# Moving the closing conditional between the last experts, gate tiles to VectorE, and weight splits to two engines

## The chip, the core and the metric

One core of one Trainium2 chip runs the whole kernel. The metric is the device time of one execution in microseconds; less is better. Three timed runs of the kernel before gave 894.11, 895.85 and 896.01 us, median 895.85. The profile is of one further execution.

## What is computed

Three layers in a row, all in float32: attention with 4 sink positions and a window of 128 keys; a dense mixture, in which every token passes all four experts; and a routed mixture, in which each token passes one of eight.

```python
x = attention(q, k, v)                      # 1536 tokens x 512
out = 0
for e in range(4):                          # dense layer, F = 1024
    h = maximum(x @ w1[e], 0)
    out += p[:, e:e+1] * (h @ w2[e])
x = out
idx = argmax(cos(x, expert_emb) / tau)      # routed layer
gate = softmax(...)[idx]
for e in range(8):
    m = idx == e
    out[m] = gate[m] * (maximum(x[m] @ w1[e], 0) @ w2[e])
```

## The kernel before

Every float32 operand of a matmul is split in two float32r halves: the high half is a cast, the low half the difference from the original. Three matmuls (high x high, high x low, low x high: SPLIT3) then give the product. Weights are loaded as raw chunks of 512 KB by SP; each chunk is split in two pieces, and each piece costs one cast (line 676 on ScalarE, 678 on another engine) and one subtraction (line 682).

**Attention and the first dense products.** The attention has a narrow path, always emitted, and a general path in a conditional at line 1464, taken only for other sinks and windows and never here. Around that conditional lie the first products of expert 0 of the dense layer, on the first 512 tokens: Moe1.first makes products 0 to 3 with their activation (ScalarE relu at line 1003, VectorE difference at 1004), then products 4 and 5 without, which stay in the two PSUM buffers of the pool psa. Moe1.again, in the conditional, makes them anew if the general path has rewritten x. Moe1.rest activates 4 and 5 and makes 6 and 7. Moe1.splits issues the weight pieces that belong to a product, on ScalarE and VectorE, and the loads that follow from freed buffers.

**Routing.** While the dense layer's last expert runs, class Route ranks tokens by expert. For each group of token tiles, gate_a to gate_e work out the gate: gate_a an inverse root on GpSimd and VectorE, gate_b and gate_c the softmax, gate_d two 128 x 96 tiles a token tile (line 933, on GpSimd), gate_e one matmul a token tile into gtab (line 940). Two groups of four come early; the last four token tiles are a joined group (a = 8, n = 4) whose gates are done late, inside the routed layer's first two slots, as the list gates_late returns.

**Routed layer.** Tokens of one expert are worked on in slots of 128. Moe2.slot is one slot: 24 matmuls of the first layer in two halves (hooks a0 to a3, b0 to b3), relu on ScalarE (1204), transposes of each half (1210, hooks t0, t1) with a copy on ScalarE (1212) and the low half on VectorE (1213), then eight products of three matmuls (1219, hooks c0 to c7). At a hook other work is emitted, so the hooks set the order on each engine's queue. An object Fill hands out the pieces of the next expert's weights one by one: the cast of a piece at one call, its subtraction and the load that its buffer allows at the next. The function busy (line 1340) chooses the engines of piece i out of 16: cast on VectorE for i = 2, 6, 11 and on ScalarE otherwise, subtraction on GpSimd for i = 0, 3, 6, 9, 12 and on VectorE otherwise.

Tokens come by an indirect DMA issued by GpSimd (gather, line 1103) into xg, are transposed by TensorE (1117) and split by ScalarE (1121) and VectorE (1122). A slot's result is scaled on ScalarE (1163) and scattered by GpSimd (1164) in flush, called at hook a3 of the next slot; gate and row numbers of a finished slot are copied by current (1173, 1174) before that.

Moe2.begin is slot 0 of expert 0, Moe2.second its slot 1, and paced every other. An expert's further slots lie in conditionals (more_slots, line 1346) that are taken by token count; in this data experts 2, 3 and 5 need one slot, 0, 1 and 7 two, 4 and 6 three. Expert e computes from one of two weight stores while the other is filled for expert e + 1. After the last slot comes flush, and after that a conditional at line 1390 whose body, overflow, would work off experts with more than three slots; it is not taken here. Where a conditional is not taken, each engine's sequencer branches over its body, waits for the engine's own outstanding work and raises its semaphores by what the body would have added. The branch hint for line 1390 is announced in announce_rest, early in the routed layer.

In the profile PE is TensorE, PEld its weight loads, DVE VectorE, ACT ScalarE, POOL GpSimd, SP the DMA queue's engine; a q behind a name is that engine's sequencer.

Of the kernel before, what the change touches and what calls it, by code (L numbers as in the profile page):

```python
# [14 lines left out]
ALU = mybir.AluOpType  # L15
# [10 lines left out]
NT = N // P  # L26
# [695 lines left out]
class Route:  # L722
# [204 lines left out]
    def gate_d(s, g):  # L927
        C, M = s.C, E2 * NT
        g["gc"] = []
        for j in range(g["n"]):  # L930
            b = s.rl.tile([P, 2, M], F32R, tag="s3", name="s3", bufs=4)
            for i, v in enumerate((g["gh"].bitcast(F32), g["gl"])):
                s.nc.gpsimd.tensor_scalar(b[:, i], C.col, g["col"][:, j : j + 1], v[:, j : j + 1], ALU.is_equal, ALU.mult)
            g["gc"].append(b)

    def gate_e(s, g):
# [46 lines left out]
class Moe1:  # L983
# [37 lines left out]

    def first(s):

        s.hs, s.ph = [], []
        for f in range(s.HELD):
            s.splits(f, False)
            s.hs.append(s.tile(f))
            s.hidden(0, f, s.hs[f])
            s.splits(f, True)
        for f in (s.HELD, s.HELD + 1):  # L1030
            s.splits(f, False)
            s.ph.append(s.product(0, f, s.psa))

    HELD = 4

    def again(s, ps):
        for f, t in enumerate(s.hs):
            s.activate(s.product(0, f, ps), t)
        for i, ph in enumerate(s.ph):
            s.again_product(0, s.HELD + i, ph)  # L1040

    def rest(s):
        for f in range(s.HELD, 8):
            s.hs.append(s.tile(f))
            i = f - s.HELD
            if i < 2:
                s.activate(s.ph[i], s.hs[f])
            else:
                s.splits(f, False)
                s.hidden(0, f, s.hs[f])  # L1050
            s.splits(f, True)


def moe1(m, nc, wts, w1, w2, wA, acc, C, pos, route, then, early):
# [94 lines left out]
class Moe2:  # L1149
# [113 lines left out]
    def second(s, w, x, fl, more):  # L1263

        hooks = {
            "start": [lambda: fl(1)],
            "a0": [lambda: fl(1)],
            "a2": [lambda: fl(1)],
            "a3": [s.flush, lambda: fl(1)],
            "t0": [lambda: fl(2)],  # L1270
            "b1": [lambda: fl(1)],
            "b2": [lambda: fl(1)],
            "t1": [lambda: fl(1)],
            "c2": [lambda: fl(2)],
            "c3": [lambda: fl(2)],
            "c5": [fl.rest, lambda: s.current(0, 1)],
        }
        for n, f in more.items():
            hooks[n] = hooks.get(n, []) + f
        s.slot(x, w, hooks)  # L1280
# [36 lines left out]
    def run(s, psT, sp, wts, hx, wAB):  # L1317
        nc, tc, R = s.nc, s.tc, s.R
        V, A, G = nc.vector, nc.scalar, nc.gpsimd
        s.psT = psT  # L1320
        x0, x1 = [sp.tile([P, 2, 4, P], F32R, name=f"xt{i}") for i in range(2)]
        xg = [sp.tile([P, D], F32, name=f"xg{i}") for i in range(2)]
        for t in xg:
            G.memset(t, 0.0)
        for c in s.stream[5:7]:
            c.buf = hx.tile([P, 1024], F32, tag="h", name="raw")
            wts.bufs.append(c.buf)
            c.load()
        nb = len(wts.bufs)
        for i, c in enumerate(s.stream[nb:]):  # L1330
            c.buf = wts.bufs[i % nb]

        def items_for(e):
            r = []
            for i in range(8 * (e - 1), 8 * e):
                a, b = s.stream[i].parts()
                r += [a + (None,), b + (s.stream[i + nb].load if i + nb < len(s.stream) else None,)]
            return r

        def busy(i):  # L1340
            return V if i in (2, 6, 11) else A, V if i % 3 or i == 15 else G


        def more_slots(e, w, ks, c):

            with ExitStack() as nest:  # L1346
                for k in ks:
                    nest.enter_context(tc.If(c > 0, label=f"more{e}_{k}", preferred_fallthrough_block=True))
                    n, more = [], {}
                    if k < ks[-1]:  # L1350
                        more["a2"] = [lambda: n.append(R.has(e, k + 1))]
                        s.gather(xg[1], e, k + 1)
                        more["c2"] = [s.split_tokens(xg[1], x1)]
                    s.paced(e, k, x1, w, Fill([], busy), more)
                    c = n[0] if n else None

        for e in range(E2):
            w = wAB[e % 2]
            nxt = e + 1 < E2
            its = items_for(e + 1) if nxt else []  # L1360
            if e == 0:
                s.gather(xg[0], 1, 0)
                s.gather(xg[1], 0, 2)
                g = s.late
                n = []
                s.second(
                    w,
                    s.x1,
                    Fill(its, busy),
                    {  # L1370
                        "start": g[1:2],
                        "a1": g[2:3],
                        "a3": g[3:4],
                        "a0": [s.announce_rest],
                        "b1": [lambda: n.append(R.has(0, 2))],
                        "c2": [s.split_tokens(xg[0], x0)],
                        "c3": g[4:5],
                        "c4": g[5:] + [s.split_tokens(xg[1], x1)],
                    },
                )  # L1380
                more_slots(0, w, range(2, CAP), n[0])
            else:
                n = []
                s.gather(xg[1], e, 1)
                if nxt:
                    s.gather(xg[0], e + 1, 0)
                s.paced(e, 0, x0, w, Fill(its, busy), {"a2": [lambda: n.append(R.has(e, 1))], "c2": [s.split_tokens(xg[1], x1)], "c4": [s.split_tokens(xg[0], x0)] if nxt else []})
                more_slots(e, w, range(1, CAP), n[0])
        s.flush()
        with tc.If(s.rest > 0, label="rest", preferred_fallthrough_block=True):  # L1390
            s.overflow(wts, wAB[0], xg[0], x0)

    def announce_rest(s):

# [3 lines left out]
    def overflow(s, wts, w, t, x):  # L1398

        nc, R = s.nc, s.R  # L1400
        for e in range(E2):
            with ExitStack() as nest:
                for k in range(CAP, NT):
                    nest.enter_context(s.tc.If(R.has(e, k) > 0))
                    if k == CAP:
                        for i, ch in enumerate(wts.chunks(*s.wb[e], w)):
                            ch.buf = wts.bufs[i % len(wts.bufs)]
                            ch.load()
                            for hi, lo in ch.parts():
                                hi(nc.scalar)  # L1410
                                lo(nc.vector)
                    s.gather(t, e, k)
                    s.split_tokens(t, x)()
                    s.slot(x, w, {})
                    s.scatter(s.po[0], s.at(R.gates, e, k), s.at(R.idx, e, k))

    def split_tokens(s, t, o):
        def f():
# [125 lines left out]
```

## Time and profile before

| | us |
|---|---|
| median of three runs | 895.85 (894.11 to 896.01) |
| the profiled execution's own time | 898.2 |
| its span in the profile | 896.4 |
| VectorE busy | 417.4 (47%) |
| ScalarE busy | 302.1 (34%) |
| GpSimd busy | 193.1 (22%) |
| mean granted TensorE clock | 0.987 of full |

Times in the profile count from the span's start. The dense products begin at 124 us, the routed layer's first slot near 678 us, and the last matmul ends near 887 us. A row of the timeline is a run of like instructions on one engine; the brackets at its end say how long the engine was idle before it and what ended that. An idle engine costs time only if TensorE, or the end of the kernel, waits for it.

### The profile page before, as it was taken

How to read it: one execution, taken by the hardware profiler on the slowest of the kernel's cores; microseconds unless marked ns; L12 is line 12 of the kernel's file. 1: busy time of each engine (PE TensorE's matmuls, PEld its weight loads, DVE VectorE, ACT ScalarE, POOL GpSimd, SP SyncE). 2: the span in 40 equal slices, each digit the busy share in tenths (PEclk: the TensorE clock that was granted, in tenths of full speed). 3: DMA queues.
4: the chain of work that ended last, by engine and by line, in shares of the span. 5: the costliest groups of instructions: out<-in, count | busy, mean ns of one | idle time of the engine just before them, and what ended most of it. 6: DMA issues, size and time to landing. Idle time of an engine off the chain costs nothing. (4 is left out here: it accounts for less than half of the span.)

```text
span 896.4 us, 11797 instructions
## 1 busy us (share of the span) xinstructions
PE 869.3 (97%) x4266; PEld 681.0 (76%) x4266; DVE 417.4 (47%) x1003; ACT 302.1 (34%) x662; POOL 193.1 (22%) x291
## 2 busy tenths in 40 slices
PE   8999999999999999999999999999999799999995
PEld 6676777878888888888888888888887577777774
DVE  5787753121233121233121234858646768937510
ACT  5787852010302010302010303111233557636421
POOL 4576510000000000000000000030223846726310
PEclk8999999999999999999999999999999999999998
DMA  7567110030022000023000022101345577946200
GB/s 135 107 137 154 46 46 2 1 119 1 0 94 94 1 0 1 1 94 94 1 1 1 0 71 84 58 0 48 118 136 170 163 254 222 307 141 205 70 32 24
DMA packets 84400, 72.47 MB, mean 81 GB/s; under 512 B 43860, under 2 KB 68436, under 8 KB 84328
## 3 DMA queue, kind: packets, MB, share of 16 engines
q1 hardware_dynamic: 81448, 65.25, 25.0%
q0 software_dynamic: 2880, 6.30, 2.1%
q8 instruction: 40, 0.66, 0.3%
q14 instruction: 32, 0.26, 0.1%
HBM read 67.58 MB, written 7.09 MB: 83 GB/s over the span
## 5 line engine op out<-in xcount | busy, mean ns | idle before, releaser
L998 PE MATMUL ph<-x,wA 128*128 128x512 f32 x1152 | 273.0, 397 | 1.5 <-DVE h L1004 1.5
L1082 PE MATMUL po<-wA,h 128*128 128x512 f32 x1152 | 273.3, 396 | 0.0
L998 PEld LDWEIGHTS ph<-x,wA 128*128 128x128 f32 x1152 | 216.5, 188 | 54.2 <-DVE h L1004 1.9
L1082 PEld LDWEIGHTS po<-wA,h 128*128 128x128 f32 x1152 | 215.1, 188 | 51.7
L1003 ACT ACTIVATE h<-ph 128x512 fp32r<-128x512 f32 x96 | 57.4, 598 | 389.4 <-PE ph L998 384.1
L1004 DVE SCALAR_TENSOR_TENSOR h<-ph,h 128x512 fp32r<-128x512 f32 x96 | 66.4, 692 | 175.9 <-ACT h L1003 175.9
L60 POOL TENSOR_TENSOR gn<-gn,rss 128x4 f32<-128x4 f32 x9 | 1.8, 198 | 444.1 <-DVE gn L58 443.6
L682 DVE TENSOR_TENSOR wA<-raw,wA 128x512 fp32r<-128x512 f32 x107 | 77.3, 750 | 2.5 <-ACT wA L676 1.7
L1092 DVE SCALAR_TENSOR_TENSOR acc<-po,pr,acc 128x512 f32<-128x512 f32 x36 | 27.0, 750 | 109.9 <-PE po L1082 109.9
L676 ACT CAST wA<-raw 128x512 fp32r<-128x512 f32 x115 | 65.5, 618 | 4.0 <-DMA raw<-in_moe_w_dram 3.6
L408 POOL TENSOR_TENSOR P<-P,r 128x264 f32<-128x264 f32 (+1 forms) x87 | 54.2, 647 | 43.9 <-DVE r L403 24.5
L1219 PE MATMUL po<-wA,ht 128*128 128x512 f32 x216 | 58.3, 409 | 0.6 <-DVE ht L1213 0.6
L1213 DVE TENSOR_TENSOR ht<-hT,ht 128x512 fp32r<-128x512 f32 x30 | 20.7, 691 | 67.9 <-ACT ht L1212 67.8
L389 ACT ACTIVATE P<-m,nm 128x264 f32<-128x264 f32 x96 | 49.0, 512 | 8.3 <-DVE nm L383 7.8
L1219 PEld LDWEIGHTS po<-wA,ht 128*128 128x128 f32 x216 | 39.7, 192 | 9.4 <-DVE ht L1213 1.5
L383 DVE CUSTOM_DVE_ANT_0 m<-sc,masks 128x264 f32<-128x264 f32 x96 | 38.5, 429 | 14.0 <-PE sc L370 12.3
L1196 PE MATMUL ph<-wA,xt 128*128 128x512 f32 x168 | 42.7, 401 | 2.0 <-PEq L1346 1.0
L682 DVE TENSOR_TENSOR wB<-raw,wB 128x512 fp32r<-128x512 f32 x44 | 40.3, 940 | 4.4 <-ACT wB L676 3.3
L771 DVE CUSTOM_DVE_ANT_0 rj<-acc,raw 128x512 f32<-128x512 f32 x64 | 40.1, 687 | 0.2
L370 PE MATMUL sc<-kk,qs 64*128 64x264 f32 x288 | 38.2, 329 | 0.7 <-DVE nm L383 0.7
L1219 PE MATMUL po<-wB,ht 128*128 128x512 f32 x144 | 38.6, 405 | 0.3 <-DVE ht L1213 0.3
L1196 PEld LDWEIGHTS ph<-wA,xt 128*128 128x128 f32 x168 | 30.6, 188 | 10.7 <-DVE xt L1122 1.9
(220 smaller groups left out, 852.1 us busy)
## 6 DMA issues: line engine op xcount, KB each, us to landing
raw<-in_moe_w_dram SPq DMA_DIRECT2D x96, 512.0 KB
vt<-in_v_dram SPq DMA_DIRECT2D x16, 192.0 KB
xs<-acc SPq DMA_DIRECT2D x12, 256.0 KB
qr<-in_q_dram SPq DMA_DIRECT2D x14, 192.0 KB
kr<-in_k_dram SPq DMA_DIRECT2D x14, 192.0 KB
raw<-en SPq DMA_DIRECT2D x4, 512.0 KB
vsr<-in_v_dram SPq DMA_DIRECT2D x64, 2.0 KB
qr<-in_q_dram SPq DMA_DIRECT2D x4, 96.0 KB
```

What stands on the lines that cost most here:

```text
L383: V.tensor_tensor_reduce(m, t["sc", par][:, :W], masks[:, VAR[i]], -1.0, 3.0e38, ALU.add, ALU.min, t["nm"][:, par, i : i + 1])
L389: A.activation(t["P"][:, par, i], t["m", par, i], AF.Exp, scale=-1.0, bias=t["nm"][:, par, i : i + 1], accum_out=t["su"][:, par, i : i + 1],)
L408: eng.tensor_tensor(y, y, t["r", a][:, par].unsqueeze(2).to_broadcast([P, b - a, W]), ALU.mult)
L676: eng.copy(dst()[:, 0], r)
L682: eng.tensor_tensor(d[:, 1], r, d[:, 0], ALU.subtract)
L771: s.nc.vector.tensor_tensor_reduce(j, s.acc[:, tt], s.eb[e], 1.0, 0.0, ALU.mult, ALU.add, s.dl[:, tt, e : e + 1])
L998: s.nc.tensor.matmul(ph, s.wA.w1(a, k, f * P)[:, :P], s.x[:, b, k, tb * TB : (tb + 1) * TB], start=(n == 0), stop=(n == 11))
L1003: s.nc.scalar.activation(t[:, 0], ph, AF.Relu)
L1004: s.nc.vector.scalar_tensor_tensor(t[:, 1], ph, 0.0, t[:, 0], ALU.max, ALU.subtract)
L1082: nc.tensor.matmul(po, hs[f][:, a, t * P : (t + 1) * P], wA.w2(b, f), start=(n == 0), stop=(n == 23))
L1196: nc.tensor.matmul(ph[b], x[:, a, kk], w.w1(c, kk, b * 512), start=(kk == 0 and n == 0), stop=(kk == 3 and n == 2),)
L1219: nc.tensor.matmul(s.po[0], ht[b][:, a, c * P : (c + 1) * P], w.w2(d, f), start=(f == 0 and n == 0), stop=(f == 7 and n == 2),)
```

## The change

Five edits. (1) In Moe1, products 0 to 5 are made ahead of the conditional, each product's activation being emitted behind the next product, so that only product 5 is held across it. (2) gate_d makes the tiles of the joined group on VectorE; gate_e, the sum of its halves and the copies of slot (0, 1) move to later hooks of second. (3) busy gives all casts to ScalarE and all subtractions to VectorE; of the routed layer's own work GpSimd keeps the indirect DMAs. (4) The conditional around overflow moves from behind the last flush to ahead of expert 7, and its body is given the weight store, token buffer and token halves that expert 7's first slot does not use. (5) overflow writes its results by flush and current like the other slots.

```diff
--- before.py
+++ after.py
@@ -930,7 +930,7 @@
         for j in range(g["n"]):
             b = s.rl.tile([P, 2, M], F32R, tag="s3", name="s3", bufs=4)
             for i, v in enumerate((g["gh"].bitcast(F32), g["gl"])):
-                s.nc.gpsimd.tensor_scalar(b[:, i], C.col, g["col"][:, j : j + 1], v[:, j : j + 1], ALU.is_equal, ALU.mult)
+                (s.nc.gpsimd if g["n"] + g["a"] < NT else s.nc.vector).tensor_scalar(b[:, i], C.col, g["col"][:, j : j + 1], v[:, j : j + 1], ALU.is_equal, ALU.mult)
             g["gc"].append(b)
 
     def gate_e(s, g):
@@ -1021,34 +1021,32 @@
 
     def first(s):
 
-        s.hs, s.ph = [], []
-        for f in range(s.HELD):
+        s.hs = []
+        for f in range(s.HELD + 1):
             s.splits(f, False)
-            s.hs.append(s.tile(f))
-            s.hidden(0, f, s.hs[f])
-            s.splits(f, True)
-        for f in (s.HELD, s.HELD + 1):
-            s.splits(f, False)
-            s.ph.append(s.product(0, f, s.psa))
-
-    HELD = 4
+            ph = s.product(0, f, s.psa)
+            if f:
+                s.finish(f - 1)
+            s.ph = ph
+
+    HELD = 5
+
+    def finish(s, f):
+        s.hs.append(s.tile(f))
+        s.activate(s.ph, s.hs[f])
+        s.splits(f, True)
 
     def again(s, ps):
         for f, t in enumerate(s.hs):
             s.activate(s.product(0, f, ps), t)
-        for i, ph in enumerate(s.ph):
-            s.again_product(0, s.HELD + i, ph)
+        s.again_product(0, s.HELD, s.ph)
 
     def rest(s):
-        for f in range(s.HELD, 8):
-            s.hs.append(s.tile(f))
-            i = f - s.HELD
-            if i < 2:
-                s.activate(s.ph[i], s.hs[f])
-            else:
-                s.splits(f, False)
-                s.hidden(0, f, s.hs[f])
-            s.splits(f, True)
+        s.finish(s.HELD)
+        for f in range(s.HELD + 1, 8):
+            s.splits(f, False)
+            s.ph = s.product(0, f, s.psa)
+            s.finish(f)
 
 
 def moe1(m, nc, wts, w1, w2, wA, acc, C, pos, route, then, early):
@@ -1273,7 +1271,7 @@
             "t1": [lambda: fl(1)],
             "c2": [lambda: fl(2)],
             "c3": [lambda: fl(2)],
-            "c5": [fl.rest, lambda: s.current(0, 1)],
+            "c5": [fl.rest],
         }
         for n, f in more.items():
             hooks[n] = hooks.get(n, []) + f
@@ -1338,7 +1336,7 @@
             return r
 
         def busy(i):
-            return V if i in (2, 6, 11) else A, V if i % 3 or i == 15 else G
+            return A, V
 
 
         def more_slots(e, w, ks, c):
@@ -1374,21 +1372,23 @@
                         "a0": [s.announce_rest],
                         "b1": [lambda: n.append(R.has(0, 2))],
                         "c2": [s.split_tokens(xg[0], x0)],
-                        "c3": g[4:5],
-                        "c4": g[5:] + [s.split_tokens(xg[1], x1)],
+                        "c4": [s.split_tokens(xg[1], x1)],
+                        "c5": g[4:5],
+                        "c7": g[5:] + [lambda: s.current(0, 1)],
                     },
                 )
                 more_slots(0, w, range(2, CAP), n[0])
             else:
                 n = []
+                if not nxt:
+                    with tc.If(s.rest > 0, label="rest", preferred_fallthrough_block=True):
+                        s.overflow(wts, wAB[1 - e % 2], xg[1], x1)
                 s.gather(xg[1], e, 1)
                 if nxt:
                     s.gather(xg[0], e + 1, 0)
                 s.paced(e, 0, x0, w, Fill(its, busy), {"a2": [lambda: n.append(R.has(e, 1))], "c2": [s.split_tokens(xg[1], x1)], "c4": [s.split_tokens(xg[0], x0)] if nxt else []})
                 more_slots(e, w, range(1, CAP), n[0])
         s.flush()
-        with tc.If(s.rest > 0, label="rest", preferred_fallthrough_block=True):
-            s.overflow(wts, wAB[0], xg[0], x0)
 
     def announce_rest(s):
 
@@ -1411,8 +1411,9 @@
                                 lo(nc.vector)
                     s.gather(t, e, k)
                     s.split_tokens(t, x)()
+                    s.flush()
                     s.slot(x, w, {})
-                    s.scatter(s.po[0], s.at(R.gates, e, k), s.at(R.idx, e, k))
+                    s.current(e, k)
 
     def split_tokens(s, t, o):
         def f():
```

## Rows read from the trace of the kernel before

**Rows 1.** Busy time of the engines, first part of the page.

```profile
PE 869.3 (97%) x4266; PEld 681.0 (76%) x4266; DVE 417.4 (47%) x1003; ACT 302.1 (34%) x662; POOL 193.1 (22%) x291
```

**Rows 2.** Who TensorE waited for, 680 to 897 us and first layer: us in total, times, longest.

```profile
PE hT L1210 <- DVEq L1346: 3.1, 1, 3.1
...
PE gtab L940 <- POOL s L933: 2.2, 2, 1.2
...
PE ph L998 <- DVE h L1004: 1.5, 1, 1.5
...
PE ph L1196 <- DVE xt L1122: 1.4, 3, 0.6
...
PE ph L1196 <- PEq L1346: 1.3, 4, 0.4
...
PE po L1219 <- DVE ht L1213: 0.9, 3, 0.3
```

**Rows 3.** Timelines of ScalarE and TensorE at line 1464: start us, us, idle before.

```profile
141.43 0.60 ACT L1003 ACTIVATE h<-ph 128x512 fp32r<-128x512 f32 x1 [3.57 <-PEq L1464]
...
142.81 5.88 PE L998 MATMUL ph<-x,wA 128*128 128x512 f32 x24 [1.50 <-DVE h L1004]
```

**Rows 4.** Lines 933 (stretch 684 to 712) and 893: count, duration ns min/median/max.

```profile
L933 POOL TENSOR_SCALAR s<-colc,gcol,ggl x4: 676/1142/1600, 698.4 to 704.1; 128x96 fp32r<-128x96 f32 x4
...
L893 DVE TENSOR_SCALAR s<-colc,gcol,tok x12: 318/324/350, 599.9 to 681.8; 128x96 fp32r<-128x96 f32 x12
```

**Rows 5.** Timelines of VectorE and GpSimd in the second slot of expert 0.

```profile
697.34 0.69 DVE L1213 TENSOR_TENSOR ht<-hT,ht 128x512 fp32r<-128x512 f32 x1 [3.01 <-ACT ht L1212]
...
704.28 5.90 DVE L678 CAST wB<-raw 128x512 fp32r<-128x512 f32 x1
...
704.89 5.00 POOL L682 TENSOR_TENSOR wB<-raw,wB 128x512 fp32r<-128x512 f32 x4
```

**Rows 6.** Stretches: length, PE, PEld, DVE, ACT, POOL busy, granted clock, DMA share, GB/s.

```profile
689.90:710.20 20.30, 17.98 (x68) 13.32 (x68) 14.89 (x21) 10.78 (x22) 18.58 (x22) 0.83 0.41 129
...
705.10:708.60 3.50, 3.50 (x11) 2.85 (x12) 3.50 (x1) 1.00 (x3) 3.50 (x3) 0.51 0.39 106
...
739.90:753.40 13.50, 13.39 (x64) 10.41 (x64) 10.75 (x13) 10.56 (x20) 8.30 (x6) 1.00 0.66 189
```

**Rows 7.** Timelines of TensorE and ScalarE in the first slot of expert 1.

```profile
710.31 3.74 PE L1196 MATMUL ph<-wB,xt 128*128 128x512 f32 x15
...
717.12 0.63 PE L1210 MATMUL hT<-ident,hh 128*128 128x128 f32 x4 [3.07 <-DVEq L1346]
...
715.06 0.62 ACT L676 CAST wA<-raw 128x512 fp32r<-128x512 f32 x1 [2.04 <-DMA raw<-in_moe_w_dram]
...
715.59 0.59 ACT L1204 ACTIVATE hh<-ph 128x512 f32<-128x512 f32 x1
```

**Rows 8.** Timelines of ScalarE, TensorE, VectorE, GpSimd around expert 2.

```profile
739.68 2.18 ACT L676 CAST wB<-raw 128x512 fp32r<-128x512 f32 x4 [3.00 <-PEq L1346]
...
743.09 0.60 ACT L1204 ACTIVATE hh<-ph 128x512 f32<-128x512 f32 x1 [1.22 <-issue]
...
746.53 0.60 ACT L1204 ACTIVATE hh<-ph 128x512 f32<-128x512 f32 x1
...
747.73 0.60 PE L1210 MATMUL hT<-ident,hh 128*128 128x128 f32 x4
...
754.68 1.89 DVE L682 TENSOR_TENSOR wB<-raw,wB 128x512 fp32r<-128x512 f32 x3
...
753.74 1.32 POOL L1103 DMA_INDIRECT xg<-xs,ridx  x1 [1.19 <-PEq L1346]
```

**Rows 9.** The kernel's end: last scatter, its landing (us), sequencers' lines 1390 and 1530.

```profile
888.37 0.98 POOL L1164 DMA_INDIRECT out_dram<-os,curt  x1 [8.57 <-ACTq L1390]
...
out_dram<-os,curt POOLq DMA_INDIRECT x1, 3.1
...
L1390 PEldq COMPARE_BRANCH  x1: 458/458/458, 887.7 to 887.7; - x1
...
L1390 POOLq INC_SWDGE_SEM  x1: 894/894/894, 891.6 to 891.6; - x1
...
L1530 POOLq DRAIN  x3: 46/109/3017, 892.5 to 896.1; - x3
```

## The prediction

> **What bounds the kernel now.** I read the busy table first: TensorE is busy for 869.3 us of a span of 896.4 us, and no other engine for half of it [rows 1]. So only the 27 us in which TensorE stands still are to be had, and the second view is who it waited for. That view names nearly all that this change touches [rows 2]: 3.1 us once for VectorE's sequencer at line 1346 (the conditional around further slots), 2.2 us in two waits for GpSimd's gate tiles (line 933), 1.5 us in the first layer (line 998), 1.4 us for token splits (line 1122), 1.3 us in four waits for TensorE's own sequencer at line 1346, and 0.9 us for line 1213. What follows the last matmul no wait of TensorE tells. I then read the engines' timelines around each of these.
>
> **First layer.** Products 4 and 5 lie in both PSUM buffers across the conditional at line 1464. ScalarE takes product 4 only once TensorE has passed that conditional, at 141.43, after 3.57 us idle; VectorE follows, and TensorE starts product 6 at 142.81, 1.50 us late [rows 3]. A product lasts 5.88/2 = 2.9 us [rows 3], so product 4 had lain ready that long. After the change it is taken ahead of the conditional while product 5 is being made: the two halves of the activation, a cast and a subtraction, each 0.6 to 0.7 us and two to an engine, inside 2.9 us. Its buffer is free when product 6 wants it. What is late next is TensorE's own passing of the conditional, elsewhere 1.3 us in four times [rows 2], 0.3 us. The weight pieces and their three loads keep their order on ScalarE, VectorE and SP. Term: 0.3 - 1.5 = **-1.2** (ends 0, if x, which the conditional's body could write, makes TensorE wait as long as now; and -1.5).
>
> **Gate tiles.** GpSimd makes eight tiles for the last four token tiles, four of them at 1.14 us in the median [rows 4], and TensorE's gate matmuls after the fourth product of the second slot's second layer wait 2.2 us for the last two pairs [rows 2]. The change makes them on VectorE, whose tile of the same shape took 0.32 us [rows 4]: eight are 2.6 us, queued ahead of the split of the hidden half. There VectorE stood idle 3.0 us for ScalarE [rows 5], which covers them; without that cover they would cost up to 2.6 us. The four gate matmuls go two products later, the total and the copies of gate and token numbers to the slot's end; the scatter that reads these comes half a slot later, so TensorE meets no new wait. Term: **-2.2** (ends -2.2 and 2.6 - 2.2 = +0.4).
>
> **Clock.** Right after that wait TensorE was granted half its clock, 1.2 GHz in place of 2.4, around 705.1 to 708.6 [rows 6]. It worked through all 3.5 us of it, so the stretch cost 1.7 us. With the wait gone it should be at full clock. But the three timed runs differ among themselves by 1.9 us, about one such stretch, so perhaps not every run has it: I take half, **-0.85** (0 to -1.7).
>
> **The wait of 3.1 us.** A VectorE cast lasted 5.90 us, from 704.28, while GpSimd was in four weight subtractions from 704.89 to 709.9 [rows 5]; so VectorE reached line 1346 late. After the change GpSimd subtracts no weights and VectorE casts none. From the second slot's start VectorE then has 16 subtractions at 0.6 [rows 8], four hidden and token splits at 0.7, the eight tiles and about 2 us of small gate work: some 17 us. TensorE's second slot is 17.98 us of work with 1.7 of half clock in it [rows 6], so 16.3, and it asks for VectorE only after the first 15 matmuls of the next slot, 3.74 us [rows 7]: VectorE is in time by 3 us. What is late next is ScalarE: its relu there stood behind a cast that waited 2.04 us for raw weights, and ended at 716.18, where TensorE went on at 717.12 [rows 7]. Those loads were late because GpSimd, busy with gate tiles, freed their buffers late; VectorE frees them sooner. Term: **-3.05** (ends -0.9, if the relu stays as late; and -3.1).
>
> **Seven weight changes.** Of each expert's 16 pieces, 5 were subtracted on GpSimd and 3 cast on VectorE; now ScalarE casts 16 and VectorE subtracts 16. Casts follow each other at (2.18 - 0.62)/3 = 0.52 us [rows 7, 8], subtractions at (1.89 - 0.69)/2 = 0.60 [rows 5, 8]. ScalarE: 16 x 0.52 + seven others at 0.5 to 0.6 = 12 us; VectorE: 16 x 0.6 + 4 x 0.6 + 0.3 = 12.3 us; a slot of TensorE takes 13.4 [rows 6]. Both fit. The extra cast ahead of the first relu meets 1.22 us of idle time. The extra cast ahead of the second moves its end from 747.13 to 747.65, and TensorE transposes it at 747.73: just in time [rows 8]. Experts 2, 3 and 5 have a single slot for it; behind them lie the 1.4 and 0.9 us that TensorE waits for VectorE [rows 2]. I take most of these 2.3 us back, **-1.9**. Ends: -2.3; and +6, if each of three gathers a slot blocked VectorE for its 1.3 us, which makes 16.2 us of work in 13.4, thrice, less the 2.3 paid now. Against that end stands a gather at 753.74, beside which three subtractions ran on undisturbed, 1.89 us for all [rows 8].
>
> **The conditional, moved.** Between experts 6 and 7 every engine now branches over the overflow body, and TensorE passes once more: **+0.3**, as above. Expert 7's second gather queues behind that on GpSimd; a gather that waited for such a passing, at 753.74 [rows 8], held nobody up. SP has no loads left there, and the body is given the other buffers, so the first slot's tokens and weights are not its to hold. Ends: 0, and 0.3 plus the 0.46 us that TensorE's branch took at the kernel's end [rows 9], 0.76. The Trainium skill ("Runtime: NRT & Kernel Launch", Instruction fetch mechanics) states that a taken branch whose target is not in the window of instructions at hand stops the engine until it is fetched. By that the term would be at its upper end and the sum 0.46 us higher; no run here yet shows the branch in that place.
>
> At the end the last scatter is issued at 888.37 and lands 3.1 us later. GpSimd, in the conditional, waits for that, then spends 0.89 us on a DMA semaphore and 3.02 us, from 892.5, draining [rows 9]; 0.9 us later the span ends. Without the conditional GpSimd drains right after the issue, at 889.4: with 3.0 and 0.9 the end is 893.3. If a drain of 3 us follows the landing all the same, it is 895.4. The other two drains took 0.05 and 0.11 us [rows 9], so the long one finishes what the conditional left, and I take the early end: **-3.1** (ends -1.0 and -3.1).
>
> **Sum.** -1.2 - 2.2 - 0.85 - 3.05 - 1.9 + 0.3 - 3.1 = -12.0 us. The profiled execution took 898.2, 2.35 above the median of the runs; the terms are differences within it, and I set them against the median: 895.85 - 12.0 = **883.85 us**, say 883.8.
>
> **Rivals.** (a) The closing conditional is not what holds the tail, and moving it does not do what it says: the drain follows the landing. For it: no drain without the conditional is in the trace. The tail then gives 1.0: 885.9. (b) ScalarE takes VectorE's place: the 3.05 shrinks to 0.9 because raw weights land late, and the 1.9 stays, as its casts stand ahead of each relu. For it: the 2.04 us of [rows 7]. Against: the idle time ahead of the relu in [rows 8]. 883.8 + 2.15 + 1.9 = 887.9. (c) Slower: ScalarE, alone with the casts, stands at each of the seven weight changes as in [rows 7], 2.04 us, with relu and hidden copy behind it: 7 x 2.04 = 14.3, so 898.1. It decides from 12.0/7 = 1.7 us a slot on. Against: only that one slot, whose loads GpSimd had held up, shows such a wait.
>
> **Numbers.** Forecast 0.58, (a) 0.20, (b) 0.13, (c) 0.06, an outcome within 0.2% (about 1.8 us, what a measurement can tell) 0.03. Faster 0.91, same 0.03, slower 0.06. The range goes from 879.5, all terms at their good ends and some of the profile's own 2.35 us, to 890.5, which holds (b) and the clock and half of the branch at their bad ends.
>
> **What would show it.** Right: product 6 within 0.4 us of product 5's end; no wait on line 933 or for VectorE at 1346; no half clock near 705; line 682 on VectorE alone, at 0.68 us; one more wait for TensorE's sequencer, 0.3 us, ahead of expert 7; under 6.5 us from last matmul to end of span. Wrong: new waits of TensorE for ScalarE's relu or copies, subtractions stretched beside gathers, or a drain of 3 us that starts after the landing.

## The result and the profile after

The change makes the kernel **884.38 us** (median of four runs, 883.79 to 885.37) against 895.93 for the kernel before (894.11 to 897.24): ratio **0.9862**, interval 0.9844 to 0.9881. The forecast was 883.8, range 879.5 to 890.5. The profiled execution took 883.79, its span is 882.0 us, 14.4 less than that of before; the medians differ by 11.55.

The busy table of the kernel after answers to [rows 1]:

```profile
PE 865.5 (98%) x4266; PEld 678.6 (77%) x4266; DVE 403.2 (46%) x1025; ACT 312.8 (35%) x683; POOL 136.0 (15%) x248
```

TensorE's busy time falls by only 3.8 us; for the rest of the 14.4 us it had stood still in the kernel before, or had already ended. What is left of its waits from 680 us on answers to [rows 2] (us in total, times, longest):

```profile
PE ph L1194 <- ACTq L1344: 1.5, 4, 0.4
PE xT L1115 <- DMA g<-xs,ridx: 1.0, 1, 1.0
PE ph L1194 <- ACT xk L1119: 0.7, 1, 0.7
PE ph L1194 <- PEq L1344: 0.4, 1, 0.4
PE ph L1194 <- PEq L1384: 0.3, 1, 0.3
```

The lines have moved by two (1346 is now 1344, 1196 is 1194, 1390 is 1384). Every wait on which the prediction rested is gone: for VectorE's sequencer, the gate tiles, the token splits, the low hidden halves. What stays are the joins of conditionals, 0.3 to 0.4 us each (a join is the point behind a conditional at which an engine goes on), and the wait for a gather and the copy of its rows, which the change doesn't touch. TensorE's timeline shows the four places (start us, us, idle before); they answer to [rows 3, 7, 8]:

```profile
140.44 5.85 PE L998 MATMUL ph<-x,wA 128*128 128x512 f32 x24 [0.30 <-PEq L1465]
...
704.42 3.77 PE L1194 MATMUL ph<-wB,xt 128*128 128x512 f32 x15 [0.37 <-ACTq L1344]
...
731.23 3.77 PE L1194 MATMUL ph<-wA,xt 128*128 128x512 f32 x15 [0.43 <-PEq L1344]
...
850.02 3.74 PE L1194 MATMUL ph<-wB,xt 128*128 128x512 f32 x15 [0.30 <-PEq L1384]
```

Product 6 stands 0.30 us behind product 5, no longer 1.50. The slot that follows expert 0's second begins 0.37 us behind it, and its transposes wait for nobody. The row at 850.02 shows the price of the conditional in its new place, 0.30 us. The gate tiles, by line 933 (duration ns min/median/max), answer to [rows 4]:

```profile
L933 DVE TENSOR_SCALAR s<-colc,gcol,ggh x4: 320/322/364, 692.0 to 693.4; 128x96 fp32r<-128x96 f32 x4
L933 DVE TENSOR_SCALAR s<-colc,gcol,ggl x4: 321/322/324, 692.2 to 693.7; 128x96 fp32r<-128x96 f32 x4
```

The clock by stretches (length, then busy time of each engine, granted clock, DMA share, GB/s) answers to [rows 6]:

```profile
690.00:691.00 1.00, 1.00 (x4) 0.80 (x3) 0.90 (x5) 0.25 (x1) 0.71 (x1) 0.50 0.14 51
...
698.00:703.00 5.00, 5.00 (x31) 4.31 (x32) 4.19 (x8) 4.39 (x9) 1.03 (x1) 1.00 0.79 233
703.00:708.00 5.00, 4.63 (x20) 3.27 (x18) 4.19 (x10) 4.50 (x9) 1.27 (x1) 1.00 1.05 338
```

The stretch at 1.2 GHz near 705 is gone; another, behind the gather wait (689 to 692.6 us, 691.5 to 694.9 before), stays. The end, by line 1531 (GpSimd's sequencer) and GpSimd's timeline, answers to [rows 9]:

```profile
L1531 POOLq DRAIN  x3: 50/120/4392, 876.7 to 881.7; - x3
```
```profile
876.95 0.98 POOL L1162 DMA_INDIRECT out_dram<-os,curt  x1 [8.55 <-ACT os L1161]
```

GpSimd's drain begins at 876.72, even before the last scatter is issued, and ends at 881.11, 3.2 us after the issue's end; the span ends 0.9 us later. From the last matmul to the end it is 6.15 us, in place of 9.17.

### The profile page after: what moved, and what is told of

Its sections match the earlier page's. It is cut to its first block, busy times and chain, and to the rows that moved or that the text cites. A ratio compares the mean times of both kernels' runs of the same rounds, so it can differ in the third digit from the quotient of the medians.

```text
span 882.0 us, 11784 instructions
## 1 busy us (share of the span) xinstructions
PE 865.5 (98%) x4266; PEld 678.6 (77%) x4266; DVE 403.2 (46%) x1025; ACT 312.8 (35%) x683; POOL 136.0 (15%) x248
## 5 line engine op out<-in xcount | busy, mean ns | idle before, releaser
L676 ACT CAST wA<-raw 128x512 fp32r<-128x512 f32 x124 | 70.0, 618 | 0.4 <-ACTq L1344 0.4
L1217 PE MATMUL po<-wA,ht 128*128 128x512 f32 x216 | 56.5, 402 | 0.0
```

Of the source, the lines that this page charges most:

```text
L676: eng.copy(dst()[:, 0], r)
L1217: nc.tensor.matmul(s.po[0], ht[b][:, a, c * P : (c + 1) * P], w.w2(d, f), start=(f == 0 and n == 0), stop=(f == 7 and n == 2),)
```

## Experiments

Two lengths are read from every trace: **main**, from the first dense product (line 998) to the end of the last matmul, and the **tail** from there to the span's end. Main leaves out the attention, whose end alone differs between 121.8 and 127.3 us over the profiled executions, more than most edits are worth. The kernel before has main 763.04 and tail 9.17, the kernel after 752.78 and 6.15. Where one run is named, the kernel before took 892.68 in a run beside it, and 898.48 (median) beside the one without the last scatter.

### The four parts, each alone on the kernel before

Their four kernels ran in turn with the kernel before (median 898.5 on that chip). The first layer's part:

```diff
-        for f in range(s.HELD):
+        for f in range(s.HELD + 1):
             s.splits(f, False)
...
+            ph = s.product(0, f, s.psa)
+            if f:
+                s.finish(f - 1)
...
```

> The kernel before with the edit of the first layer alone (products made ahead, product 5 alone held). Theory: the wait of 1.50 us ahead of product 6 shrinks to TensorE's own passing of the conditional, 0.3 us, and nothing else moves: 1.2 us faster, ratio about 0.9987. Rival (x, which the body could write, holds product 6 as long): a wait of 1.5 us stays, ratio 1.000.

Measured: 899.6 us, ratio 0.9994 (0.9974 to 1.0015; the ratio compares all runs, and its median here lies above that of the kernel before). Main is 761.72, 1.3 less. The gap ahead of the product behind the conditional is 0.41 us in place of 1.50, and the waits from 680 us on are those of the kernel before. So the part gives its 1.1 to 1.2 us, less than these runs can tell from nothing.

The gate tiles:

```diff
-                s.nc.gpsimd.tensor_scalar(b[:, i], ...
+                (s.nc.gpsimd if g["n"] + g["a"] < NT else s.nc.vector).tensor_scalar(b[:, i], ...
...
-                        "c3": g[4:5],
-                        "c4": g[5:] + [s.split_tokens(xg[1], x1)],
+                        "c4": [s.split_tokens(xg[1], x1)],
+                        "c5": g[4:5],
+                        "c7": g[5:] + [lambda: s.current(0, 1)],
```

> The kernel before with the gate tiles on VectorE and the gate matmuls, sum and copies at later hooks; GpSimd keeps its five subtractions an expert. Theory: the wait of 2.2 us on line 933 and the stretch at half clock behind it go (3.9 us in the trace), and since GpSimd is no longer late with its subtractions the wait of 3.1 us at line 1346 shrinks under 1 us: 5 to 6.5 us faster. Rival (the 3.1 us come from GpSimd's subtractions as such, not from their lateness): that wait stays, 3 to 4 us faster.

Measured: 896.44 us, ratio 0.9994 (0.9968 to 1.002); main is 761.07, 2.0 less. Neither expectation came: the wait at line 1346 falls from 3.1 to 2.5 us only, and nothing of 3 to 6.5 us is won. The wait on line 933 is gone, but another stands in its place, which no step of the prediction had named. VectorE's timeline, then GpSimd's, then TensorE's:

```profile
694.30 1.63 DVE L933 TENSOR_SCALAR s<-colc,gcol,ggh 128x96 fp32r<-128x96 f32 x1
...
696.34 2.13 DVE L933 TENSOR_SCALAR s<-colc,gcol,ggl 128x96 fp32r<-128x96 f32 x1
```
```profile
694.54 1.31 POOL L682 TENSOR_TENSOR wB<-raw,wB 128x512 fp32r<-128x512 f32 x1
...
697.11 1.28 POOL L682 TENSOR_TENSOR wB<-raw,wB 128x512 fp32r<-128x512 f32 x1
```
```profile
700.07 1.55 PE L1219 MATMUL po<-wA,ht 128*128 128x512 f32 x4 [2.47 <-DVE ht L1213]
```

Two of the eight tiles last 1.63 and 2.13 us, the other six 0.32. Each long one ends within 0.1 us of the end of a GpSimd subtraction (695.85, 698.39). The low hidden half behind them comes late, TensorE waits 2.47 us for it, and the half clock moves there (0.50 from 700.7 to 704.1). The part alone trades one wait for another.

The engines of the weight pieces:

```diff
-            return V if i in (2, 6, 11) else A, V if i % 3 or i == 15 else G
+            return A, V
```

> The kernel before with all casts on ScalarE and all subtractions on VectorE; gate tiles stay on GpSimd at their old hooks. Theory (GpSimd's subtractions block VectorE): no VectorE instruction of line 682 over 1 us, the waits of 1.4 and 0.9 us for token and hidden splits behind experts 2, 3 and 5 go, the wait of 3.1 us goes, the wait on line 933 shrinks from 2.2 to about 1 us: 6 to 7 us faster. Rival (VectorE or ScalarE has too much to do now): waits of TensorE for lines 1122, 1213 or 1204 stay or grow, under 3 us faster.

Measured: 894.03 us, ratio **0.9939** (0.9913 to 0.9965). Main is 757.44, 5.6 less. The waits for VectorE's sequencer, the token splits and the low halves are all gone. The waits view and the stretch behind the gate matmuls show what comes instead:

```profile
PE gtab L940 <- POOL s L933: 3.4, 2, 1.7
```
```profile
706.20:713.00 6.80, 6.20 (x17) 4.76 (x17) 3.34 (x7) 2.14 (x4) 2.79 (x3) 0.50 0.63 205
```

GpSimd's gate tiles, now beside VectorE's sixteen subtractions, reach 1.88 us, the wait for them grows from 2.2 to 3.4 us where about 1 was expected, and the half clock behind it from 3.5 to 6.8. So each of the two parts has a cost alone that the other removes.

The conditional (and with it the body's new flush and current):

```diff
+                if not nxt:
+                    with tc.If(s.rest > 0, label="rest", preferred_fallthrough_block=True):
+                        s.overflow(wts, wAB[1 - e % 2], xg[1], x1)
...
-        with tc.If(s.rest > 0, label="rest", preferred_fallthrough_block=True):
-            s.overflow(wts, wAB[0], xg[0], x0)
```

> The kernel before with the closing conditional moved ahead of expert 7. Theory: GpSimd's drain of about 3 us follows the issue of the last scatter in place of its landing and the DMA semaphore, 3.0 us less from last matmul to end of span; TensorE passes once more ahead of expert 7, 0.45 us: 2.5 us faster. Rival (instructions behind the branch have to be fetched by TensorE there): 1 us or more of a wait ahead of expert 7, 2 us faster or less.

Measured: 895.24 us, ratio **0.9961** (0.9939 to 0.9983). The tail is 6.13, 3.04 less; main is 763.25, with one new gap of 0.30 us ahead of expert 7. Ahead of expert 2, where no edit of this part lies, this execution had other waits than the kernel before: 3.6 us for the gate tiles in place of 2.2, with half clock for 6.8 us in place of 3.5, and 1.8 us for ScalarE's relu (line 1204) in place of the 3.1. Why, no row tells. At the end of the kernel the part stands by itself.

In main the four parts alone make -1.3 - 2.0 - 5.6 + 0.2 = -8.7 us; together they make -10.3. But these executions are not alike in the clock behind the gather. The kernel before, the kernel after and the first layer's part lost some 1.7 us of main there to a stretch at half clock; the other three parts had none. The kernel before, then the part with the weight engines:

```profile
691.50:694.90 3.40, 3.40 (x9) 2.64 (x8) 2.55 (x8) 0.41 (x1) 2.91 (x4) 0.50 0.66 227
```
```profile
692.00:694.00 2.00, 1.99 (x7) 1.12 (x8) 1.63 (x5) 1.11 (x4) 1.63 (x5) 1.00 0.91 334
694.00:696.00 2.00, 2.00 (x10) 1.47 (x8) 1.86 (x8) 0.99 (x3) 1.66 (x2) 1.00 0.55 187
```

Counted alike, the parts make by estimate -1.3 - 0.3 - 3.9 + 1.9 = -3.6 us, and 6.7 us are missing to -10.3, of which the other waits in the conditional's execution are a part. The timed runs give the four parts 0.06, 0.06, 0.61 and 0.39%, 1.1% in all, against 1.4% together, with about 0.2% of doubt on each. So how much the parts gain by each other stays open; that the gate tiles and the weight engines do is shown by the waits above and below.

### Parts taken back from the kernel after

Gate tiles on GpSimd again, at the late hooks (line 933 as in the kernel before):

> The changed kernel with the eight gate tiles back on GpSimd, gate matmuls, sum and copies at the new late hooks. Theory (the late hooks and a GpSimd free of subtractions do it, the engine matters little): tiles of 0.7 to 1.9 us on GpSimd are done 14.8 us into the second slot, about when TensorE comes to the gate matmuls; a wait on line 933 under 0.5 us, no stretch at half clock, span within 1 us of the changed kernel. Rival (the tiles must leave GpSimd): waits on line 933 of 1 us or more and half clock behind them, 1 to 3 us longer.

Measured: 881.83 us in one run, main 752.10. TensorE waits for the tiles once:

```profile
PE gtab L940 <- POOL s L933: 1.7, 1, 1.7
```

But in this execution the clock is full from 11.4 us on, at the gather too, whose wait is only 0.30 us. The 1.7 us lost here and the stretch that this run was spared are of one size, so the time alone says nothing; the row says that the engine of the tiles is worth 1.7 us. Behind this wait the clock stayed full, which neither expectation had.

VectorE's three casts back, GpSimd still without weights:

```diff
-            return A, V
+            return V if i in (2, 6, 11) else A, V
```

> The changed kernel with the three casts of an expert back on VectorE, all subtractions on VectorE too, so GpSimd still has indirect DMAs alone. Theory (what held VectorE was GpSimd's subtractions): casts of 0.42 us, none over 1 us, VectorE has 12.3 + 3 x 0.4 = 13.5 us of work a slot of 13.4, so waits for lines 1120 and 1211 of at most 0.5 us behind the one-slot experts; within 1.5 us of the changed kernel. Rival (VectorE's casts are what is held, by indirect DMAs too): casts of 1 us and more and waits of 2 us and more in all.

Measured: 883.93 us in one run, main 751.92. VectorE's casts, by line 678:

```profile
L678 DVE CAST wB<-raw x12: 416/418/420, 691.9 to 823.5; 128x512 fp32r<-128x512 f32 x12
L678 DVE CAST wA<-raw x9: 417/419/420, 709.0 to 809.5; 128x512 fp32r<-128x512 f32 x9
```

Not one of 21 is stretched, with gathers and scatters still on GpSimd. (This execution was at full clock behind the gather, which is worth 1.7 us of its main.) Behind the one-slot experts TensorE waits for no split; in expert 1's first slot 0.93 and 0.41 us for VectorE come back, and the joins behind two one-slot experts are 0.30 in place of about 0.4. So VectorE's casts cost about 1 us, and none of them is held up when GpSimd does no subtractions.

GpSimd's five subtractions back, all casts on ScalarE:

```diff
-            return A, V
+            return A, V if i % 3 or i == 15 else G
```

> The changed kernel with the five subtractions of an expert back on GpSimd, all casts on ScalarE. Theory (a subtraction with two inputs on GpSimd blocks VectorE's subtractions and gate tiles as well as its casts): subtractions of 1.3 to 3 us on VectorE, waits for lines 1120 and 1211 behind experts 2, 3 and 5 and a wait in the second slot come back, 3 us or more longer than the changed kernel. Rival (the casts alone were held): VectorE stays near 0.69 us an instruction and the span within 1 us.

Measured: 897.58 us in one run; main is 762.37, 9.6 more than in the kernel after, although the clock was full behind the gather here. TensorE's waits, VectorE's timeline and GpSimd's:

```profile
PE po L1217 <- DVE ht L1211: 3.5, 1, 3.5
PE hT L1208 <- DVEq L1344: 2.3, 1, 2.3
```
```profile
695.90 2.13 DVE L933 TENSOR_SCALAR s<-colc,gcol,ggl 128x96 fp32r<-128x96 f32 x1
...
698.43 3.35 DVE L933 TENSOR_SCALAR s<-colc,gcol,ggh 128x96 fp32r<-128x96 f32 x1
```
```profile
696.64 1.32 POOL L682 TENSOR_TENSOR wB<-raw,wB 128x512 fp32r<-128x512 f32 x1
...
699.20 2.50 POOL L682 TENSOR_TENSOR wB<-raw,wB 128x512 fp32r<-128x512 f32 x2
```

A tile of 0.32 us lasts 3.35 and ends at 701.78, 0.08 behind two subtractions of GpSimd. VectorE's own subtractions are held up too, up to 3.49 us in place of 0.68. The half clock is back for 6.8 and 3.4 us:

```profile
701.80:708.60 6.80, 5.45 (x17) 4.47 (x18) 4.37 (x9) 2.49 (x5) 0.78 (x1) 0.50 0.53 163
718.90:722.30 3.40, 3.25 (x10) 2.80 (x11) 2.76 (x5) 2.77 (x6) 1.69 (x2) 0.50 0.81 203
```

Behind the one-slot experts TensorE waits three times 0.3 us again for the splits. So nearly all that the weight change brings, it brings by taking GpSimd's subtractions away. The Trainium skill ("SBUF — State Buffer", Who interferes with whom) says that VectorE and GpSimd share one pair of ports, and that the one that issues first holds it for its whole instruction while the other stands; a cast or a tensor_scalar of VectorE can need the pair. The rows agree that VectorE is held up: its casts and tiles took 0.42 us (the kernel with the casts back) and 0.32 us (the kernel after) without GpSimd's subtractions beside them, 5.90 [rows 5] and 3.35 us with them. They add two things. The 5.90 us passed beside four subtractions and the 3.35 beside two, so the price is not bounded by one instruction. And in the kernel before eight tiles of line 893 ran at 0.32 to 0.35 us beside GpSimd's own gate tiles (line 933 near 600 and 647 us), so not every arithmetic of GpSimd holds them up.

The conditional left out (this kernel would not work off experts with more than three slots; there is none in this data):

```diff
-                if not nxt:
-                    with tc.If(s.rest > 0, label="rest", preferred_fallthrough_block=True):
-                        s.overflow(wts, wAB[1 - e % 2], xg[1], x1)
```

> The changed kernel without the closing conditional anywhere; it leaves out the work on experts with more than three slots, of which this data has none. Theory: the 0.30 us ahead of expert 7 go, 0.45 us from start to start, and the stretch from last matmul to end of span stays at 6.2 us. Rival (the conditional's place in the middle costs through fetching or queues too): 1 us or more shorter ahead of expert 7.

Measured: 885.0 us in one run. There is no gap ahead of expert 7, and main is 751.58, 0.5 to 1.2 less than in the two executions of the kernel after (752.12, 752.78). The tail is 6.14. So the conditional costs about half a microsecond in the middle and nothing at the end.

The last slot's scaling and scatter left out:

```diff
-        s.flush()
+        pass
```

> The changed kernel without the last flush: the result of the last slot is neither scaled nor scattered. Theory (GpSimd's drain lasts until about 3.2 us after the issue of its latest indirect DMA has ended): with the latest one 9 us earlier the drain is under 0.2 us, the span ends 1 to 1.5 us after the last matmul in place of 6.2 us. Rival (a drain of 3 us belongs to the kernel's end): the span ends 4 us or more after the last matmul.

Measured: 880.53 us in one run; the tail is 1.27 us. By the drain's line:

```profile
L1531 POOLq DRAIN  x3: 50/114/4761, 870.3 to 878.4; - x3
```

The long drain is still there. It starts at 870.27, 0.25 us behind the last indirect DMA that is left, lasts 4.76 us and is over at 875.03, while TensorE works until 877.43. So a drain of 3 to 5 us stands behind the last indirect DMA whether a conditional comes before it or not, against the expectation of 0.2 us. It ends 5.0 us behind the issue's end here, 3.2 in the kernel after, so no fixed time from the issue fits both. The last slot's scaling and scatter, with the drain behind them on the path, cost 6.15 - 1.27 = 4.9 us.

### The clock behind the gather

The kernel after, once more, and the same with 28 spare matmuls of 128 columns around the gather wait (their PSUM columns are read by nobody):

```diff
-            s.transposed(s.g1, s.x1)()
+            warm(16)
+            split = s.transposed(s.g1, s.x1)
+            warm(12)
+            split()
```

> The changed kernel itself, to set the next one beside it on the same chip: 0.986 to 0.990 of the kernel before.

> The changed kernel with 16 matmuls of 128 columns in bfloat16 on constants ahead of the transposes of the second slot's tokens and 12 behind them, into unused PSUM columns, where TensorE waits 1.0 us for the gathered rows and 0.7 us for their copy. Theory (the half clock at 689 follows from these waits): the granted clock stays full there and 3.4 us at half clock are saved to 1.7 us. Rival (matmuls of that kind do not keep the clock, or they come late and hold the transposes): the stretch at half clock stays and the span is the same or up to 0.5 us longer.

Measured: 886.43 us (ratio 0.9854, 0.9822 to 0.9886) and 885.64 us (0.9849, 0.9823 to 0.9875). The stretch from the ranking's first matmul to the end of expert 0's slots, in the repeated kernel and in the other:

```profile
680.04:706.79 26.75, 25.47 (x117) 19.16 (x116) 20.33 (x57) 15.74 (x31) 9.92 (x22) 0.94 0.61 195
```
```profile
680.91:706.24 25.33, 25.29 (x145) 19.59 (x144) 20.28 (x57) 15.75 (x31) 9.94 (x22) 1.00 0.66 207
```

The clock stays at 2.4 GHz and the stretch is 1.42 us shorter; but the time doesn't show it. TensorE's timeline, and its sequencer by line 1392, the conditional around overflow:

```profile
852.90 3.74 PE L1195 MATMUL ph<-wB,xt 128*128 128x512 f32 x15 [1.26 <-PEq L1392]
```
```profile
L1392 PEldq COMPARE_BRANCH  x1: 3201/3201/3201, 849.4 to 849.4; - x1
```

Ahead of expert 7 TensorE now stands for 1.26 us in place of 0.30, since its sequencer takes 3.20 us over the branch that takes 0.33 in the kernel after. The last kernel has half the spare matmuls, 8 and 6:

> The kernel after with 14 spare matmuls (8 and 6) in TensorE's idle time ahead of the second slot's gather, in place of 28. F, the 1.26 us ahead of expert 7 comes of where the instructions lie, which 56 more on TensorE had moved: with 28 more the gap there takes another value between 0.3 and 1.3 us, and the time is that of the run with 28 less what the gap is shorter. C, the 1.26 was chance: the gap is 0.30 as in the kernel after, the time 1 us under that of the run with 28. For both: if 14 do as well as 28 for the clock, no stretch at half clock behind 30 us and the passage from the ranking's first matmul to the second slot's start in 25.3 us; if they don't, the stretch near 690 us is back, 26.7 us, and the time is the kernel after's. Best case 1.5 us under the kernel after, ratio to the kernel before 0.984.

Measured: 883.16 us (880.34 to 886.92), ratio **0.9818** (0.9795 to 0.9842). The same stretch, TensorE's timeline and its sequencer at the slots' conditionals (line 1352):

```profile
681.21:706.72 25.51, 24.70 (x131) 18.84 (x130) 20.37 (x57) 15.72 (x31) 10.26 (x22) 1.00 0.65 203
```
```profile
748.62 1.64 PE L1195 MATMUL ph<-wB,xt 128*128 128x512 f32 x6 [1.17 <-PEq L1352]
```
```profile
L1352 PEldq COMPARE_BRANCH  x16: 68/194/4269, 703.4 to 879.2; - x16
```

With fourteen the clock is full too. That the spare matmuls did it is not shown: of the twelve profiled executions without them six had full clock behind the gather as well. The gap ahead of expert 7 is 0.30 us, which alone would fit chance as well; but the long branch has not gone, it has moved: 4.27 us, at the join ahead of expert 3, where TensorE stands 1.17 us in place of 0.4. In the other twelve traces no branch of TensorE in the routed layer takes over 0.46 us. A branch that takes 3 to 4 us appears only where instructions were added on TensorE, and at another conditional with another number of them. That suggests their place in the program and speaks against chance; one profiled execution of each kernel is all there is for it. The Trainium skill ("Runtime: NRT & Kernel Launch", Instruction fetch mechanics), by which a taken branch stops the engine while its target is fetched if that is not at hand, would make such a difference; what was at hand no row tells. This version is 1.8% under the kernel before. Against the kernel after it was not run on one chip, its interval meets that of the repeated run, and main in its profiled execution is only 0.4 us shorter (751.73 against 752.12). That it is faster is not shown.

## Why the prediction was right, step by step

Each term, as predicted and as the two profiled executions of before and after show it (us):

| step | predicted | measured |
|---|---|---|
| first layer | -1.2 | -1.2 |
| gate tiles | -2.2 | -2.2 |
| clock near 705 | -0.85 | -1.7 |
| the wait of 3.1 | -3.05 | -2.85 |
| seven weight changes | -1.9 | -3.25 |
| the conditional, moved | +0.3 | +0.46 |
| the end | -3.1 | -3.0 |
| sum | -12.0 | -13.75 |

Beside these, the attention ended 1.15 us earlier and the gather wait was 0.44 longer, neither of the change; with them the sum is -14.5, and the spans differ by 14.4. The profiled execution of before lay 2.3 above its median and that of after 0.6 below, so the medians show 11.55, and 12.05 in the repeated run. That 884.38 lies only 0.6 from the forecast is in part luck: within the two profiled executions the terms made 1.75 us more than forecast, the clock and the weight changes above all, and that the two profiled executions lie 2.9 us further apart than the medians hides it.

**First layer, gate tiles, the wait of 3.1.** As predicted, with the successors that were named: 0.30 us for the passing of the conditional, no wait at the later gate matmuls, and a join of 0.37 us where the 3.1 had been. The cover for the gate tiles, VectorE's idle 3.0 us, held. What the steps left out is that they are not separate: the gate tiles at 0.32 us need a GpSimd that does no subtractions, which the gate tiles' single part shows from one side (2.47 us of new wait) and the taking back of the subtractions from the other (3.5). The tile's duration was taken from a row of another stretch [rows 4], in which GpSimd did no weights. It was right only because the third edit makes that so here too.

**Clock.** Half a stretch was taken, because perhaps not every run had it. In the profile it was whole, 1.7 us. How many of the timed runs of before had it, their times don't tell. The term also shows that the prediction's opening was too narrow: it gave only the 27 us in which TensorE stands still as to be had, but work at half clock counts as busy. And the wait alone doesn't explain the stretch: with the tiles back on GpSimd TensorE waited 1.7 us at the same matmuls and kept its full clock.

**Seven weight changes: the size was off.** The waits were counted by the gaps that the profile prints, 2.3 us for six. Between 731.23 and 849.73 experts 2 to 6 take 118.50 us, before from 739.93 to 861.68 121.75. The ends of matmuls are modelled: one is shown 0.40 us long, while in a run they start every (3.74 - 0.40)/14 = 0.24. A gap is counted from such an end, so 0.16 us of every wait lies under the matmul before it: 6 x 0.16 = 1.0 us. The Trainium skill ("Perfetto Trace Analysis", Tensor Engine Instruction) says as much, that this engine's ends are estimates. A further 0.4 of the 1.35 missing is what the prediction had left of the 2.3 as a guess; the joins took back 0.3, and 0.2 stays open. The conditional's 0.46 is likewise its printed 0.30 and 0.16. ScalarE and VectorE carried their 16 pieces as worked out; the joins behind the one-slot experts ask for ScalarE now, at about 0.4 us in place of 0.30.

**The end: the size was right and the reason wrong.** The 3.02 us of drain were put down to what the conditional had left. But the drain lasts 4.39 us in the kernel after, 4.38 with the conditional's move alone and 4.76 where the last scatter is left out. What went is the wait for the landing and the 0.89 us of INC_SWDGE_SEM ahead of the drain: the drain now runs from before the issue on.

**The rivals.** (a) The drain after the landing: it ends 1.5 us behind the landing (879.58), not 3, and the tail is 6.15, not 8.2. (b) ScalarE late: its relu holds nobody up in expert 1's first slot in the kernel after (0.34 us once, in the kernel without the last scatter). (c) ScalarE at every weight change: no wait of 1.7 us or more at any of the seven, only the joins of about 0.4.

## What to carry to other kernels

Before work moves to an engine, ask which third engine's instructions ran beside it where its duration was read: a tile of 0.32 us became 3.35 beside a neighbour's subtractions, and two edits of which each alone brought a new or longer wait (2.47 and 3.4 us) had neither together. Before parts are compared by one profiled execution each, see whether they ran at the same clock. Ending a kernel with an indirect DMA and no conditional behind it saved 3 us. Count stalls of TensorE from start to start of its matmuls, not by the printed gaps, and look at every conditional again after adding instructions, since a branch that is hidden at 0.3 us took 3 to 4 in two kernels here, and TensorE then stood for 1.2.

## What the runs showed that was not expected

- A drain of 3 to 5 us stands at the kernel's end in every order that was run: 3.02 us with all landed, 4.4 where it starts 0.2 us ahead of the last scatter, 4.76 right behind an earlier one.
- Blocking reaches through small instructions: in the single gate part the total price of two blocked tiles was (1.63 - 0.32) + (2.13 - 0.32) = 3.1 us on VectorE, and TensorE paid 2.47 of it.
- TensorE's clock falls behind some waits and not behind others: without spare matmuls it was full behind the gather after waits of 0.30, 0.43, 0.55, 0.62, 0.68 and 0.84 us, and half after 0.40, 0.56, 0.58, 1.00, 1.05 and 1.15 us. So the length of the wait doesn't decide it, and what does stays open.
- A branch of TensorE's sequencer took 3.20 and 4.27 us in two kernels with added instructions, and at most 0.46 in all others.
